# One load instead of two for the first heads' keys and for w_o's first rows, in a decode step on one core

## The chip, the core and the metric

The kernel runs on one core of a Trainium2 chip. A core has a matrix engine (TensorE, in the profile PE, with its weight loads as PEld), a vector engine (VectorE, DVE), a scalar engine (ScalarE, ACT), GpSimd (POOL) and SyncE (SP), which here only waits for semaphores and issues loads. Sixteen DMA engines move the data. The metric is the time of one execution on the device in microseconds (us): the median of several runs.

## What is computed

One token (a row x of 576) goes through two branches, whose results are added to x. Cut to what matters:

```python
xn = layernorm(x)
# A: attention over the last W = 4096 positions of a cache, 32 query heads, 16 key/value heads of 128
q = xn @ wq                                  # wq: 576 x 4096
p = softmax(q . k[last 4096] * 128**-0.5)    # each key head serves two query heads
A = (p . v[last 4096]) @ wo                  # wo: 4096 x 576
# B: gated MLP
z = gelu(xn @ w_in)                          # w_in: 576 x 4608, halves z1 and z2
B = (z1 * (layernorm(z2) * w_sp + b_sp)) @ w_out   # w_out: 2304 x 576
out = x + A + B
```

There is one token, so every weight is used once and every cached key and value by two query heads: 51 MB are read for some 40 million multiplications.

## The kernel before

**Tiles and stages.** The 16 key heads are worked in four stages b = 0 to 3 of four heads each (`NB = 4`, `HB = 4`). The keys of a stage are one tile k0, k1, k2 or k3 of 128 partitions x 32 KB (4096 KB), the values likewise v0 to v3. Of each partition's 128 positions, line 214 (`turn`) transposes 16 at a time, so a stage's keys take eight transposes on VectorE. `scores(b)` multiplies them with the queries on TensorE (line 259), takes the maximum on VectorE (line 262 to 275), the exponential on ScalarE (line 279), and turns the result with a ninth transpose (line 281). `values(b)` multiplies with the values (line 293) and normalizes (line 304). `z_all` and `gate` are the MLP's first half; at the end stand the output rows: o_p (line 375) holds the attention's result, and lines 391 and 399 multiply it with w_o's 32 rows per partition and the gate's hv with w_out's 18.

**Order.** The schedule is written by hand: every engine runs its instructions in program order. The order of the stages is turn 0, scores 0, turn 1, scores 1, values 0, turn 2, scores 2, values 1, turn 3, scores 3, gate, values 2, values 3, then the output rows. VectorE and TensorE alternate inside a stage.

**Loads.** SyncE issues all large loads in the order in which lines 106 to 124 list them: w_q in three pieces, k0 in two halves (line 107), k1, v0, k2, v1, k3, w_in in two, v2, v3, w_o's rows 0 to 13 and 14 to 27 (line 120), its last four rows (wo28), and w_out in five pieces. ScalarE issues three tiny ones (x and two scalars). Large tiles share two buffers, small ones (k0 to k3, v2 and w_o's first 28 rows are of this width) share two more. So a load can have to wait until an earlier tile's readers are done: k2 takes the buffer of k0 and waits for k0's last transpose, k3 that of k1, v1 that of w_q, w_in that of v0, v2 that of k2, v3 that of v1, w_o's first 28 rows that of k3, w_out that of w_in. While SyncE waits for one, all loads behind it wait too.

**Semaphores.** Each load and the store of the result adds to one of eight semaphores on completion; the DMAs take these eight in turn, in the order of the program. A DMA whose turn comes on a semaphore waits until the DMA eight places before it has landed. A reader waits until its load's semaphore has its full count, which is after the whole of that one load. In the profile's records the eight have the numbers 100, 102, 103, 104, 106, 107, 109 and 110. Before, there are 26 DMAs, and the store is the last of them and sits on 102. At the end SyncE waits for all semaphores, two in each instruction, before the closing barrier of the engines.

The names: `load` and `load_kv` cut a tile's columns at `cuts` and issue one DMA for each piece; NU = 128 positions a partition, WR = 32 rows of w_o a partition, D = 576.

Of the kernel before, what the change touches and what calls it, by code (L numbers as in the profile page):

```python
# [15 lines left out]
D = 576  # L16
# [9 lines left out]
NU = W // NJ  # L26
# [11 lines left out]
SMALL = NU * DH  # L38
# [6 lines left out]
def kernel(  # L45
# [38 lines left out]
    def unit(name, width):  # L84
        pool = small if width == SMALL else large
        return pool.tile([P, width], BF16, name=name, tag="u")
# [4 lines left out]
    def load(t, view, width, cuts):  # L91
        for a, e in zip(cuts, cuts[1:]):
            nc.sync.dma_start(t[:, (a - cuts[0]) * width:(e - cuts[0]) * width], view[:, a * width:e * width])  # L93

    def load_kv(cache, name, b, width, cuts=(0, NU)):
        t = unit(f"{name}{b}", width)
        src = cache[0, HB * b:HB * (b + 1), SK - W:SK, :].rearrange("s (j u) d -> j s (u d)", u=NU)
        for a, e in zip(cuts, cuts[1:]):
            nc.sync.dma_start(t[:, a * DH:e * DH], src[:, :, a * DH:e * DH])  # L99
        return t  # L100

    kn, vn = {}, {}
    wq_v, win_v = halves(A_wq), halves(B_w_in)
    wo_v = A_wo.rearrange("(p r) n -> p (r n)", r=WR)
    wq_t = unit("wq", LARGE)
    load(wq_t, wq_v, 2048, (0, 2, 4, NR))
    kn[0] = load_kv(A_k_cache, "k", 0, SMALL, (0, NU // 2, NU))
    kn[1] = load_kv(A_k_cache, "k", 1, SMALL)
    vn[0] = load_kv(A_v_cache, "v", 0, LARGE)
    kn[2] = load_kv(A_k_cache, "k", 2, SMALL)  # L110
# [6 lines left out]
    vn[2] = load_kv(A_v_cache, "v", 2, SMALL)  # L117
    vn[3] = load_kv(A_v_cache, "v", 3, LARGE)
    wo_t = unit("wo", SMALL)
    load(wo_t, wo_v, D, (0, 14, 28))  # L120
    wo28 = one.tile([P, FH], BF16, name="wo28", tag="side")
    load(wo28, wo_v, D, (28, WR))
    wout_t = unit("wout", LARGE)
# [285 lines left out]
    nc.sync.dma_start(out.flatten_outer_dims().rearrange("o (g c) -> (o g) c", g=4), res[0:97:32, :])  # L409


# [1 line left out]
_INS = ['A_x', 'A_k_cache', 'A_v_cache', 'A_wq', 'A_wo', 'B_x', 'B_w_in', 'B_w_sp', 'B_b_sp', 'B_w_out']  # L413
_OUTS = [((1, 1, 576), 'bfloat16')]
# [25 lines left out]
```

## Time and profile before

| | us |
|---|---|
| median of 3 runs (lowest, highest) | 128.26 (128.17, 128.54) |
| the profiled execution's own time | 128.43 |
| its span, first to last instruction | 126.6 |
| busy: TensorE matmul, VectorE, ScalarE | 76.3, 65.6, 10.2 |
| share of 16 DMA engines' span, SyncE's queue | 94.8% |
| SyncE issues k0's halves | 2.09 and 2.87 |
| first transpose of k0, last one's end | 19.12, 28.65 |
| SyncE issues k2 | 28.67 |
| SyncE issues w_o's first piece | 83.19 |
| last load landed | 123.25 |
| SyncE issues the store | 123.97 |

A time in the profile counts from the span's first instruction. The page gives busy time by engine, the busy share of engines and DMA in 40 slices, the DMA queues, and the chain of work that ended last: from the last instruction back, at each step, to what released it. A transfer in this chain counts from its issue to its landing, so that a transfer that waits in the queue behind others is long there. The timeline lists instructions in order, with the idle time of the engine before each and what ended it. SyncE's waits are events of its own sequencer, and their times are in the semaphore records.

### The profile page before, as it was taken

Reading aid. Unit: us, or ns where it says so; the run is one execution under the profiler, and the core shown is the slowest. Engines: PE = TensorE matmul, PEld = TensorE weight load, DVE = VectorE, ACT = ScalarE, POOL = GpSimd, SP = SyncE. Lnnn points to the kernel's source line nnn. Section 1 sums busy time; section 2 is a strip of 40 time slices with the busy share of each in tenths; the row PEclk is TensorE's granted clock in tenths of the full one; section 3 lists DMA queues with packets and bytes.
Section 4 is the critical chain, followed back from the end, with each engine's and each line's share of the span. In section 5 each row is a group of like instructions: output and inputs, shape, how many; then the busy total and the mean of one; then the engine's idle time right before and its main releaser. Section 6 shows DMA issues by size and latency. Waiting matters only on the chain.

```text
span 126.6 us, 1380 instructions
## 1 busy us (share of the span) xinstructions
PE 76.3 (60%) x562; PEld 35.0 (28%) x562; DVE 65.6 (52%) x133; ACT 10.2 (8%) x19; POOL 3.9 (3%) x10
## 2 busy tenths in 40 slices
PE   3241435995179946339963729991960865757470
PEld 3120211331023413313422403330730432423240
DVE  6660069996599844079953169944438400040010
ACT  4010000000300003100003100003000110100010
POOL 8400000000000000000000000000000000000000
PEclk9999999999756999955999975698555595865555
DMA  4999999998998999989999899898999989999930
GB/s 101 427 445 440 430 424 450 430 497 383 448 471 352 476 404 435 476 362 476 404 435 476 382 459 454 384 454 387 487 393 440 455 366 418 433 405 423 400 138 0
DMA packets 3187, 51.03 MB, mean 403 GB/s; under 512 B 365, under 2 KB 622, under 8 KB 1134
## 3 DMA queue, kind: packets, MB, share of 16 engines
q1 hardware_dynamic: 3176, 50.96, 94.8%
q8 instruction: 4, 0.07, 0.2%
q14 instruction: 1, 0.01, 0.0%
q10 hardware_dynamic: 6, 0.00, 0.0%
HBM read 50.96 MB, written 0.00 MB: 402 GB/s over the span
## 4 chain that ended last, share of the span: by engine, by line
DMA 78%; PE 10%; DVE 6%; SPq 2%; ACT 1%; issue 1%; ACTq 0%
DMA k<-in_A_k_cache_dram 37%; DMA v<-in_A_v_cache_dram 27%; DMA wout<-in_B_w_out_dram 14%; PE s L259 8%; DVE kt L214 5%; PE pv L293 1%; ACT p L279 1%; SPq L93 1%; SPq L99 1%; DVE sm L262 1%; PE tr L270 0%; PE su L283 0%; PE fin L399 0%; DVE res L408 0%; DVE m L272 0%
## 5 line engine op out<-in xcount | busy, mean ns | idle before, releaser
L259 PE MATMUL s<-kt,zq 128*128 128x512 bf16 x128 | 38.4, 465 | 10.3 <-DVE kt L214 10.1
L214 DVE STREAM_TRANSPOSE kt<-k 128x1024 f32<-128x1024 f32 x32 | 36.6, 1208 | 3.1 <-DMA k<-in_A_k_cache_dram 3.1
L259 PEld LDWEIGHTS <-zq 128*128 128x128 bf16 x128 | 14.6, 114 | 32.9 <-issue 23.0
L293 PE MATMUL pv<-v,pt 128*32 128x512 bf16 x128 | 10.2, 477 | 1.9 <-DMA v<-in_A_v_cache_dram 1.9
L279 ACT ACTIVATE p<-sm,nm 128x1024 bf16<-128x1024 f32 x4 | 4.6, 1147 | 71.1 <-DVE nm L275 71.1
L304 DVE TENSOR_TENSOR o_t<-op,rm 128x8 bf16<-128x8 f32 x4 | 0.7, 166 | 15.0 <-PE op L301 15.0
L223 PE MATMUL q_ps<-wq,xw 128*32 128x512 bf16 x36 | 4.2, 627 | 6.6 <-DMA wq<-in_A_wq_dram 4.3
L262 DVE CUSTOM_DVE_ANT_1 sm<-s,cm 128x512 f32<-128x512 f32 x8 | 5.4, 672 | 4.7 <-PE s L259 4.7
L281 DVE STREAM_TRANSPOSE pt<-p 128x1024 bf16<-128x1024 bf16 x4 | 5.0, 1245 | 5.4 <-ACT p L279 5.4
L283 PE MATMUL su<-sel,l 128*128 128x8 f32 x8 | 1.8, 293 | 7.6 <-ACT p L279 7.6
L301 PE MATMUL op<-selu,pvs 128*128 128x8 f32 x32 | 4.2, 259 | 2.8 <-ACT pvs L298 2.8
L293 PEld LDWEIGHTS <-pt 128*32 128x32 bf16 x128 | 3.7, 118 | 6.6 <-issue 3.2
L301 PEld LDWEIGHTS op<-selu,pvs 128*128 128x128 f32 x32 | 3.9, 191 | 4.8 <-ACT pvs L298 4.8
L391 PE MATMUL acc<-wo,o_p 128*1 128x288 bf16 x64 | 4.4, 439 | 0.8 <-DMA wo<-in_A_wo_dram 0.8
L395 DVE COPY acc_sb<-acc 128x288 f32<-128x288 f32 x1 | 0.5, 459 | 8.4 <-PE acc L391 8.4
L227 DVE CAST q_sb<-q_ps 128x512 bf16<-128x512 f32 x1 | 0.7, 692 | 7.5 <-PE q_ps L223 7.5
L317 PE MATMUL z<-win,xw 128*32 128x288 bf16 x72 | 4.5, 446 | 0.0
L270 PE MATMUL tr<-ident_f,m 128*128 128x128 f32 x8 | 1.9, 326 | 3.9 <-DVE m L268 3.9
L223 PEld LDWEIGHTS <-xw 128*32 128x32 bf16 x36 | 1.4, 130 | 8.6 <-issue 8.6
L283 PEld LDWEIGHTS su<-sel,l 128*128 128x128 f32 x8 | 1.4, 218 | 8.4 <-ACT p L279 8.4
L298 ACT COPY pvs<-pv 128x512 f32<-128x512 f32 x4 | 2.3, 586 | 13.0 <-PE pv L293 13.0
L346 PE MATMUL sz_ps<-sz,ones_f 128*128 128x2 f32 x2 | 0.6, 362 | 4.6 <-DVE sz L343 4.6
(95 smaller groups left out, 45.1 us busy)
## 6 DMA issues: line engine op xcount, KB each, us to landing
v<-in_A_v_cache_dram SPq DMA_DIRECT2D x4, 4096.0 KB, 32.3
k<-in_A_k_cache_dram SPq DMA_DIRECT2D x3, 4096.0 KB, 30.6
win<-in_B_w_in_dram SPq DMA_DIRECT2D x1, 4608.0 KB, 34.2
k<-in_A_k_cache_dram SPq DMA_DIRECT2D x2, 2048.0 KB, 19.1
wo<-in_A_wo_dram SPq DMA_DIRECT2D x2, 2016.0 KB
wq<-in_A_wq_dram SPq DMA_DIRECT2D x1, 2560.0 KB, 12.6
wq<-in_A_wq_dram SPq DMA_DIRECT2D x2, 1024.0 KB, 6.9
wout<-in_B_w_out_dram SPq DMA_DIRECT2D x1, 1152.0 KB, 25.3
```

The source lines that it names most:

```text
L214: nc.vector.transpose(t[:].rearrange("p c n e -> p (c n e)").bitcast(FP32), kn[b][:, UK * DH * k:UK * DH * (k + 1)].bitcast(FP32).rearrang ...
L223: nc.tensor.matmul(q_ps[32 * g:32 * g + 32, :], lhsT=xw[:, r, :], rhs=wq_t[:, 2048 * r + 512 * g:2048 * r + 512 * (g + 1)], start=r == 0, ...
L259: nc.tensor.matmul(s_ps[:], lhsT=zq[:, b, ce, ZPAD - 8 * k4:ZPAD - 8 * k4 + P], rhs=kt[b, 4 * kk + k4][:, c, :, e], start=k4 == 0 and ce = ...
L262: nc.vector.tensor_tensor_reduce(out=sm[:, kk, :].rearrange("p (n s) -> p n s", s=HB), in0=s_ps[:].rearrange("p (n s) -> p n s", s=HB), in ...
L279: nc.scalar.activation(p[:], sm[:].rearrange("p k n -> p (k n)"), ACT.Exp, bias=nm[:], accum_out=l[:])
L281: nc.vector.transpose(p_t[b][:].rearrange("p k u m -> p (k u m)"), p[:])
L283: nc.tensor.matmul(su[:], lhsT=l[:].to_broadcast([P, P]), rhs=sel8[:], start=True, stop=True)
L293: nc.tensor.matmul(pv[32 * g:32 * g + 32, :].rearrange("p (n d) -> p n d", n=4), lhsT=p_t[b][:, kk, u, :], rhs=v4[:, kk, u, :, :], start=k ...
L298: nc.scalar.copy(pvs[:], pv[:])
L301: nc.tensor.matmul(op[:], lhsT=pvs[:, DH * u:DH * (u + 1)], rhs=selu[:, 8 * u:8 * u + 8], start=u == 0, stop=u == 3)
L317: nc.tensor.matmul(zp[i][32 * g:32 * g + 32, :], lhsT=xw[:, r, :], rhs=rhs, start=r == 0, stop=r == NR - 1, tile_position=(0, 32 * g))
L391: nc.tensor.matmul(acc[i][32 * g:32 * g + 1, :], lhsT=col, rhs=w[:, HW * i:HW * (i + 1)], start=n == 0 and g > 0, stop=n + 4 >= len(rows), ...
```

## The change

Two loads that were issued in two pieces are issued in one. The halves of k0 become one load of 4096 KB, so that its readers wait for one semaphore and for the whole tile. The two 14-row pieces of w_o become one load of 28 rows, 4032 KB. The bytes, the tiles, the buffers and all compute instructions stay. There are 24 DMAs instead of 26; all DMAs behind the first cut move up by one place in the turn of semaphores, those behind the second by two, and the store comes to 110, the last of the eight.

```diff
-    kn[0] = load_kv(A_k_cache, "k", 0, SMALL, (0, NU // 2, NU))
+    kn[0] = load_kv(A_k_cache, "k", 0, SMALL)
...
-    load(wo_t, wo_v, D, (0, 14, 28))
+    load(wo_t, wo_v, D, (0, 28))
```

## The prediction

> **What bounds the kernel now.** I read the page first, then the chain of waits in order of time, then the timeline, then SyncE's closing instructions. The page:
>
> ```profile
> DMA  4999999998998999989999899898999989999930
> q1 hardware_dynamic: 3176, 50.96, 94.8%
> DMA 78%; PE 10%; DVE 6%; SPq 2%; ACT 1%; issue 1%; ACTq 0%
> ```
>
> The second line is the queue of all SyncE's loads: 50.96 MB, and its packets fill 94.8% of the 16 DMA engines' span. The chain names DMA for 78%, and the rest of it is mostly work by which a buffer came free for a load that then waited in a full queue. The chain's DMA pieces and its end:
>
> ```profile
> 2.87 21.13 DMA k<-in_A_k_cache_dram
> 24.02 4.63 DVE kt L214 x4
> 28.67 25.92 DMA k<-in_A_k_cache_dram
> ...
> 71.19 34.61 DMA v<-in_A_v_cache_dram
> 105.80 0.02 issue
> 105.82 17.43 DMA wout<-in_B_w_out_dram
> 123.25 0.04 issue
> 123.29 0.32 PE fin L399 x4
> ```
>
> A load of 4096 KB is issued 26 to 35 us before it lands. Alone it takes 9.71 us: by the semaphore records the loads of k0 (second half), k1, v0, k2, v1 and k3 land at 23.99, 33.70, 44.87, 54.58, 64.30 and 74.01, one behind the other (v0's 11.17 us hold a 1.1 us instruction fetch at 36.8 on one DMA engine, which keeps that engine behind from then on). So the bound is one unbroken stream of loads to 123.25, then a tail of 3.4 us to the span's end at 126.6. The profiled execution took 128.43 us, 1.8 around its span; the median of the runs is 128.26. I take the sum as a difference and subtract it from 128.26.
>
> The places where compute waits for the stream are the slack that the change can use:
>
> ```profile
> 24.02 4.62 DVE L214 STREAM_TRANSPOSE kt<-k 128x1024 f32<-128x1024 f32 x4 [0.27 <-DMA k<-in_A_k_cache_dram]
> 54.61 9.13 DVE L214 STREAM_TRANSPOSE kt<-k 128x1024 f32<-128x1024 f32 x8 [1.91 <-DMA k<-in_A_k_cache_dram]
> 74.03 9.13 DVE L214 STREAM_TRANSPOSE kt<-k 128x1024 f32<-128x1024 f32 x8 [0.94 <-DMA k<-in_A_k_cache_dram]
> 105.85 3.18 PE L293 MATMUL pv<-v,pt 128*32 128x512 bf16 x32 [1.92 <-DMA v<-in_A_v_cache_dram]
> 112.88 1.84 PE L391 MATMUL acc<-wo,o_p 128*1 128x288 bf16 x26
> 115.48 2.56 PE L391 MATMUL acc<-wo,o_p 128*1 128x288 bf16 x38 [0.76 <-DMA wo<-in_A_wo_dram]
> 119.70 1.13 PE L391 MATMUL acc<-wout,hv 128*1 128x288 bf16 x16 [1.65 <-DMA wout<-in_B_w_out_dram]
> 121.48 0.77 PE L399 MATMUL fin<-wout,hv 128*1 128x144 bf16 x20 [0.65 <-DMA wout<-in_B_w_out_dram]
> ```
>
> The bracket is the engine's idle time before the row and what ended it.
>
> **Part 1, two transfers fewer in the stream: -0.15 us.** The halves of k0 land at 19.10 and 23.99, after wq's last piece at 14.21: 4.89 and 4.90 us, together 9.79. The undivided 4096 KB of k1, k2, v1 take 9.71 to 9.72. One cut costs 0.075 us. The packet records say why: a 16384 B packet takes 611 ns, a 32768 B one 1214 to 1219, so two cost 3 to 8 ns more than one, 8 times per DMA engine, and a 4-byte packet of 9 ns ends each transfer. wo's halves take 4.82 each (v3 lands at 105.80, they at 110.62 and 115.44), 9.64; a line through 4096 KB in 9.71 and 576 KB (wo28) in 1.43 gives 9.56 for 4032 KB, again 0.077 less. From below it could be 2 x 0.04 (8 packets x 4 ns + 9), from above 2 x 0.09; I take 0.15. It reaches the end undiminished as long as the queue never runs dry. SyncE's two issues (728 and 333 ns) lie beside the stream.
>
> The Trainium skill (DMA: Bandwidth & Descriptors, Anatomy of one DMA) gives each DMA on the gpsimd queue a fixed part of about 2.0 us besides its bytes; by that as an estimate two fewer would save 4 us. The rows of this stream differ: 0.075 us each.
>
> **Part 2, the store on the last semaphore: -0.19 us.** SyncE's closing waits (L435) are event instructions that each wait for two semaphores, in a fixed order; the eight of the DMAs are 100, 102, 103, 104, 106, 107, 109, 110.
>
> ```profile
> L435 SPq EVENT_SEMAPHORE  x7: 17/28/898, 124.7 to 126.6; - x7
> SPq L435 <- DMA out_dram<-res: 0.9, 1, 0.9
> ```
>
> The semaphore records place them: (104, 103) at 124.68, (106, 102) from 124.75 to 125.64, which is the store's landing (the 898 ns), then (107, 100) at 125.68, (109, 101) at 125.74, (110, 108) at 125.80, the drain at 125.87, and the barrier. The store is the 26th DMA and sits on 102, in the second pair; three pairs pass only after it has landed, 64 ns apart. As the 24th it is on 110, in the last pair: the other four pairs take 4 x 64 = 0.26 us while the store is in flight (0.9), and the drain follows at once. Saved: 3 x 0.064 = 0.19. From below 0 (if the order of pairs changes with the counts), from above 0.26; I take 0.19 because the pairs run 3-2, 4-1, 5-0 and then 6 and 7 with engines' semaphores, an order that depends on the semaphores and not on the loads.
>
> **Part 3, k0 in one piece: VectorE starts 4.9 us later, at no cost.** Line 214's first transposes run from 19.12 on the first half. Now all eight wait for the whole, which lands at 23.92. Eight take 9.1 us (34.33 to 43.40 in k1's turn), so k0's turn ends at 33.1 instead of 28.65. What is late next: k2's load, queued behind that wait on SP with v1 behind it, is issued at 33.1 instead of 28.67; by then k1 is just landing and v0 (until 44.8) still lies ahead, so the queue stays full with 11 us to spare. scores(0)'s rest behind the transposes costs 6.3 (43.33 to 49.67 in stage 1), so k1's turn starts at 39.4 instead of 34.33, ends at 48.5, releases k3's load at 48.5 instead of 43.43 (v1 is ahead of it until 64.2), and values(0) ends 9.2 behind that: 57.7. There 1.91 us of waiting are eaten: k2's turn starts at 57.7 instead of 54.61, 3.1 late; k3's at 76.25 instead of 74.03, 2.2 late (0.94 eaten). The loads these release (win 56.0, v2 66.9, v3 74.4, wo 85.4, wo28 and wout 96.2 to 98.5) each find at least 7 us of stream ahead of them. The gate and values(2) are 2.2 late; values(3), which waited 1.92 for v3, starts at 106.2 instead of 105.85, so o_p is ready at 112.0 instead of 111.7. wo's second half landed at 115.44: 3.3 us of slack are left. The cover is the stream; without it the price would be the 4.9 itself.
>
> The loads' own waits get easier: a DMA waits until the one eight places before it has landed. v0 waited 1.5 us for wq's first piece (issued at 5.68) and now waits for x_row; wout's last piece waited for v3 (105.80) and now for v2. All lie behind a full queue: nothing.
>
> **Part 4, wo's 28 rows in one piece: 26 matmuls move behind 115.3, at no cost.** The first rows ran 112.88 to 114.72 on the first half. Now all 64 start when the whole lands at 115.3: 1.84 + 2.56 = 4.4 us at the granted clock of 0.50 that holds from 111.9 to the end, so they cannot run at a lower one that the trace has shown. They end at 119.7 against wout's first piece at 119.66 - 0.15 = 119.5: 0.2 late. PE then waits 0.65 before 121.48, and acc_sb, copied by 121.34, is first read at 122.04. Both covers hold it. From above, at the 71 ns apiece of the 26 (1.84 us) and of wout's 16 (1.13 us), 64 take 4.5 us and end 0.3 late, still under the 0.65.
>
> **The sum.** 0.15 + 0.19 = 0.34 us: the last wout lands at 123.10, the span ends at 126.28, and the time is 128.26 - 0.34 = **127.92 us**, 0.27% less.
>
> **Rivals.**
> - Only one half of the gain. The store's wait isn't the last (stream alone: 128.26 - 0.15 = 128.11), or the stream's gain is lost in the trailing DMA engine (tail alone: 128.07). For it: the pairing order is inferred from one kernel. Against: the 64 ns steps. This is also the case that the change doesn't do what it says. Chance 0.12.
> - Slower: k0's late start reaches the output matmuls. Its place is o_p (line 375) against wo's landing; it decides from 3.3 us more delay than I count. If the 4.9 us came through whole, o_p is ready at 116.6, the 64 matmuls end at about 121.9, wout's 16 at 123.0, the copies at 123.5, and 0.7 + 1.0 of line 399 follow: 125.2 instead of 123.6, so 1.6 - 0.34 = +1.3, 129.5 us. For it: DVE and PE alternate in a fixed order, and PE's granted clock falls to 0.5 in stretches of 6.8 us that may now fall on other stages. Against: 1.91, 0.94 and 1.92 us of waits in the rows. The Trainium skill (Trainium Kernel Development and Optimization, Best Practices) asks for loads that overlap compute, and this change takes such an overlap away. Chance 0.06.
> - Slower by a fetch: PE's last instruction fetch (16384 B at 119.0, 1.0 us) moves later with line 391 and meets the DMA engine that is last at 123.25: +1.0 - 0.34, 128.9 us. In the last wout load eleven engines have landed by 121.78 and five trail at 122.41, 122.92, 123.04, 123.17 and 123.25: as many as there were fetches in the span (one of 8192 B, four of 16384 B), so they hit five different engines. Chance 0.04.
> - A larger gain: an exposed start of a DMA. wq's first piece, with nothing ahead of it, needed 4.93 us from issue to landing where the next 1024 KB took 2.43; two such starts fewer would give 5.0, 123.3 us. A full queue speaks against it; 0.01. A smaller one is that the last fetch now misses the stream: down to 127.6; 0.05.
>
> **Chances.** Forecast 0.72. About 0.3% (0.38 us, under 127.88) is what a measurement of this kernel can tell from no change; the forecast lies 0.04 short of it, so I put 0.38 of its chance below and 0.34 inside. Faster: 0.38 + 0.06 = 0.44. Same: 0.34 + 0.12 + 0.02 of the slower cases where they stop early = 0.48. Slower: 0.08. The range 127.6 to 128.3 takes in the bounds of parts 1 and 2 (0.08 to 0.44 saved) and the half gain, and leaves out some 2 in 10.
>
> **What would show it.** The first transposes start at 23.9 to 24.0 and run eight in a row; k2's load is issued near 33.1. Waits of DVE for k2 and k3 vanish. DMA share stays at 9 in every slice. PE's wait for wo ends near 115.3 and takes all 64 rows. The last wout lands near 123.1. The 898 ns wait is the fifth of SyncE's closing pairs, and the drain follows within 0.05 us of it. I am wrong if a load lands later than before, if PE idles less than 0.2 us before line 399, or if pairs still follow the store's landing.

## The result, and the profile after

| | before | after |
|---|---|---|
| median, us (lowest to highest, 10 runs each) | 128.42 (128.17 to 128.54) | 127.87 (127.80 to 128.11) |
| ratio, 95% interval | | 0.9965 (0.9957 to 0.9973) |
| profiled execution: span, us | 126.6 | 126.1 |
| w_q's last piece landed, us | 14.21 | 14.11 |
| last load landed, us | 123.25 | 122.94 |
| store landed, us | 125.62 | 125.25 |

The kernel is 0.35% faster, 0.45 us by the ratio (0.34 to 0.55; the medians lie 0.55 apart); 0.34 us (0.27%) were forecast, at the edge of that interval. Ratios, here and below, leave out executions over 1.5% above their kernel's fastest, which only e7_late_4 has, six of its twelve. First the page of the changed kernel: DMA's busy share by slice, SyncE's queue, and the chain that ended last.

```profile
DMA  4999999898998989999899999899999899999940
q1 hardware_dynamic: 2888, 50.96, 94.8%
PE 42%; DMA 36%; DVE 10%; ACT 5%; SPq 3%; issue 1%; ACTq 0%
```

The stream is as full as before (94.8%), with 288 packets fewer. The chain now names TensorE for 42% where it named DMA for 78%. That isn't a new bound. The chain in order of time, near its end:

```profile
92.48 3.67 PE z L317 x72
...
96.16 0.33 SPq L93
...
98.68 0.43 SPq L93
99.11 0.04 issue
99.16 23.78 DMA wout<-in_B_w_out_dram
122.94 0.04 issue
122.98 0.26 PE fin L399 x4
```

The last load's issue came at 99.16, behind line 317, whose matmuls free w_in's buffer, and then it lay 23.78 us in a full queue. The chain follows who released the issue, and so walks through compute that had 20 us to spare. The queue's share and the full slices say what bounds.

VectorE's turns and TensorE's last part, from the timeline:

```profile
23.85 9.13 DVE L214 STREAM_TRANSPOSE kt<-k 128x1024 f32<-128x1024 f32 x8 [4.75 <-DMA k<-in_A_k_cache_dram]
38.67 9.07 DVE L214 STREAM_TRANSPOSE kt<-k 128x1024 f32<-128x1024 f32 x8
60.15 9.12 DVE L214 STREAM_TRANSPOSE kt<-k 128x1024 f32<-128x1024 f32 x8
78.46 9.12 DVE L214 STREAM_TRANSPOSE kt<-k 128x1024 f32<-128x1024 f32 x8
107.26 3.44 PE L293 MATMUL pv<-v,pt 128*32 128x512 bf16 x32
115.23 4.01 PE L391 MATMUL acc<-wo,o_p 128*1 128x288 bf16 x64 [0.61 <-DMA wo<-in_A_wo_dram]
119.44 1.13 PE L391 MATMUL acc<-wout,hv 128*1 128x288 bf16 x16 [0.20 <-DMA wout<-in_B_w_out_dram]
121.21 0.48 PE L399 MATMUL fin<-wout,hv 128*1 128x144 bf16 x20 [0.64 <-DMA wout<-in_B_w_out_dram]
```

After 23.85 no turn waits for keys any more: k1's, k2's and k3's turns carry no bracket. The waits of 1.91 and 0.94 us are eaten, as is that before line 293. TensorE still waits for w_o, 0.61 us, so the delay ends there. SyncE's closing instructions and its wait for the store:

```profile
L436 SPq EVENT_SEMAPHORE  x7: 17/28/28, 124.3 to 126.0; - x7
SPq L436 <- DMA out_dram<-res: 0.7, 1, 0.7
```

Minimum, median and maximum were 17, 28 and 898 ns and are now 17, 28 and 28. The wait for the store isn't gone. Before, the store's 102 was the second semaphore of its pair, and the wait lay inside that instruction (898 ns). Now 110 is the first of its pair, and the wait lies ahead of the instruction, from 124.53 to 125.27. The semaphore records place the pairs:

| | pairs before the store's | store landed | pairs behind it | drain | from landing to drain |
|---|---|---|---|---|---|
| before | (104, 103) | 125.62 | (107, 100), (109, 101), (110, 108) | 125.87 | 0.25 |
| after | (104, 103) to (109, 101) | 125.25 | none | 125.33 | 0.08 |

So the span's 0.53 us are: 0.09 at the start (w_q's last piece landed sooner), 0.22 in the stream from there to the last load (109.04 us before, 108.82 after), 0.06 from the last load to the store's issue (0.72, now 0.66), and 0.17 behind the store's landing.

### The profile page after: what moved, and what is told of

The parts are those of the page before. It is cut to its first block, busy times and chain, and to the rows that moved or that the text cites. A ratio compares the mean times of both kernels' runs of the same rounds, so it can differ in the third digit from the quotient of the medians.

```text
span 126.1 us, 1377 instructions
## 1 busy us (share of the span) xinstructions
PE 77.6 (62%) x562; PEld 36.3 (29%) x562; DVE 65.3 (52%) x133; ACT 10.2 (8%) x19; POOL 3.9 (3%) x10
## 3 DMA queue, kind: packets, MB, share of 16 engines
q1 hardware_dynamic: 2888, 50.96, 94.8%
## 4 chain that ended last, share of the span: by engine, by line
PE 42%; DMA 36%; DVE 10%; ACT 5%; SPq 3%; issue 1%; ACTq 0%
PE s L259 30%; DMA wout<-in_B_w_out_dram 19%; DMA k<-in_A_k_cache_dram 17%; PE pv L293 4%; ACT p L279 4%; DVE kt L214 4%; SPq L93 3%; PE z L317 3%; PE op L301 2%; DVE sm L262 2%; PE tr L270 2%; PE su L283 1%; DVE pt L281 1%; DVE m L272 1%; ACT pvs L298 1%
## 5 line engine op out<-in xcount | busy, mean ns | idle before, releaser
L259 PE MATMUL s<-kt,zq 128*128 128x512 bf16 x128 | 37.4, 460 | 11.9 <-DVE kt L214 11.9
L293 PE MATMUL pv<-v,pt 128*32 128x512 bf16 x128 | 12.6, 563 | 0.0
L301 PE MATMUL op<-selu,pvs 128*128 128x8 f32 x32 | 5.9, 311 | 2.8 <-ACT pvs L298 2.8
L301 PEld LDWEIGHTS op<-selu,pvs 128*128 128x128 f32 x32 | 5.5, 259 | 5.8 <-ACT pvs L298 5.8
L317 PE MATMUL z<-win,xw 128*32 128x288 bf16 x72 | 3.7, 382 | 0.0
```

Of the source, the lines that this page charges most:

```text
L259: nc.tensor.matmul(s_ps[:], lhsT=zq[:, b, ce, ZPAD - 8 * k4:ZPAD - 8 * k4 + P], rhs=kt[b, 4 * kk + k4][:, c, :, e], start=k4 == 0 and ce = ...
L293: nc.tensor.matmul(pv[32 * g:32 * g + 32, :].rearrange("p (n d) -> p n d", n=4), lhsT=p_t[b][:, kk, u, :], rhs=v4[:, kk, u, :, :], start=k ...
L301: nc.tensor.matmul(op[:], lhsT=pvs[:, DH * u:DH * (u + 1)], rhs=selu[:, 8 * u:8 * u + 8], start=u == 0, stop=u == 3)
L317: nc.tensor.matmul(zp[i][32 * g:32 * g + 32, :], lhsT=xw[:, r, :], rhs=rhs, start=r == 0, stop=r == NR - 1, tile_position=(0, 32 * g))
```

## The experiments

The landing times below are from the semaphore records. "Stream" is the time from the landing of w_q's last piece to that of the last load, "tail" from the store's landing to the drain. A load is spread over the 16 DMA engines, and it has landed when the last of them is done; "mean" is the stream taken from the mean of the 16 engines' landings to the same mean of the last load, so that it doesn't hang on one engine. Theory T is the forecast's: 0.077 us for each cut, about 0.06 for each pair that passes behind the store's landing, and everything else covered. Rival S puts the gain into the semaphore's place alone, rival C into k0's late start.

| kernel | ratio (95%) | median, us | w_q landed | stream | mean | tail |
|---|---|---|---|---|---|---|
| before (first profile) | | 128.42 | 14.21 | 109.04 | 108.02 | 0.25 |
| after (first profile) | 0.9965 (0.9957 to 0.9973) | 127.87 | 14.11 | 108.82 | 107.86 | 0.08 |
| e1_k0_only | 0.9990 (0.9981 to 0.9999) | 128.22 | 14.05 | 108.92 | 107.94 | 0.19 |
| e2_wo_only | 0.9984 (0.9976 to 0.9993) | 128.11 | 14.00 | 109.06 | 107.95 | 0.19 |
| e3_store_only | 0.9989 (0.9980 to 0.9997) | 128.13 | 14.21 | 109.10 | 108.02 | 0.08 |
| e4_stream_only | 0.9976 (0.9967 to 0.9985) | 127.98 | 14.14 | 108.79 | 107.68 | 0.25 |
| e5_cuts_32 | 1.0021 (1.0011 to 1.0030) | 128.67 | 14.29 | 109.55 | 108.49 | 0.08 |
| e6_late_1 | 0.9971 (0.9961 to 0.9982) | 128.11 | 14.19 | 108.94 | 107.87 | 0.08 |
| e7_late_4 | 1.0008 (0.9982 to 1.0035) | 130.18 | 14.17 | 108.85 | 107.87 | 0.08 |
| e8_wq_one | 0.9969 (0.9958 to 0.9981) | 128.01 | 14.13 | 108.78 | 107.67 | 0.08 |
| e9_k0_late | 0.9984 (0.9976 to 0.9993) | 128.14 | 14.13 | 108.87 | 107.82 | 0.25 |
| e10_wo_late | 0.9995 (0.9986 to 1.0004) | 128.29 | 14.01 | 109.13 | 108.01 | 0.25 |
| e11_after_again | 0.9963 (0.9950 to 0.9976) | 127.85 | 14.05 | 108.81 | 107.86 | 0.08 |
| e12_before_again | 1.0002 (0.9993 to 1.0011) | 128.35 | 14.07 | 109.05 | 108.02 | 0.25 |

The mean follows T's 0.077 a cut: two cuts fewer give 0.15 or 0.16 us (after, e6, e7, e11), one fewer 0.08 (e1) and 0.07 (e2), six more 0.47 (e5), and none 0.00 or 0.01 (e3, e10, e12). Three kernels lie some 0.2 us lower than T has them, e4, e8 and e9; see at k0 only late.

**One cut alone, k0's.** The diff is the change's first line only.

```diff
-    kn[0] = load_kv(A_k_cache, "k", 0, SMALL, (0, NU // 2, NU))
+    kn[0] = load_kv(A_k_cache, "k", 0, SMALL)
```

> Only k0 comes in one load; w_o's first 28 rows stay in two. 25 DMAs, the store on semaphore 100, in the third of the five closing pairs. Theory T (a cut costs the stream 0.077 us, and each closing pair that passes after the store's landing costs 0.06): k0 lands 0.08 earlier than before relative to w_q's last piece, the stream stays 0.08 ahead to its end, two pairs follow the store's landing instead of three, 0.14 us less than before in all (ratio 0.9989). Rival S (all of the gain comes from the semaphore's place, cuts cost nothing): 0.06 less (0.9995). Rival C (the late start of k0's turn, by what it moves on TensorE and in the instruction fetches, makes the gain): most of the 0.45, 0.3 to 0.45 less (0.9965 to 0.9977).

0.13 us less (0.01 to 0.24): T's number. C's 0.3 lies outside the interval, S's 0.06 doesn't. k0 lands 9.72 us after w_q, where the halves needed 9.79. Two pairs follow the store's landing, and the tail is 0.19.

**The other cut alone, w_o's.**

```diff
-    load(wo_t, wo_v, D, (0, 14, 28))
+    load(wo_t, wo_v, D, (0, 28))
```

> Only w_o's first 28 rows come in one load; k0 stays in halves, so its first transposes start near 19.1 us again. 25 DMAs, the store on semaphore 100. Theory T: w_o's 28 rows land 0.08 sooner after v3 than before, the end of the stream 0.08 sooner, two pairs behind the store's landing, 0.14 us less than before (ratio 0.9989). Rival S: 0.06 less (0.9995). Rival C: the same 0.06 or less, since nothing is late; the line-391 matmuls still start on the whole load near 115.3.

0.20 us less (0.09 to 0.31), 0.14 expected. The last landing came no sooner in this profile (a stream of 109.06), where T had 0.08; the mean of the 16 did, by 0.07. Another 0.06 lie between the last load and the store's issue (0.66 us instead of 0.72), which T didn't have. w_o's 28 rows land 9.59 us after v3, where the halves needed 9.64, and the tail is 0.19. Both rivals' 0.06 lies outside the interval of 0.09 to 0.31, as S and C gave it here.

**The store's place alone.** Two tiny loads leave, so the count comes to 24 with all cuts in place. A constant 1 stands for both scalars, w_sp and b_sp: the kernel leaves that part of the computation out.

```diff
-    nc.scalar.dma_start(ws2[:, 0:1], B_w_sp.flatten_outer_dims()[0:1, 0:1])
-    nc.scalar.dma_start(ws2[:, 1:2], B_b_sp.flatten_outer_dims()[0:1, 0:1])
...
+    nc.gpsimd.memset(ws2[:], 1.0)
```

> All cuts as before; the two 2-byte loads of w_sp and b_sp are left out and a constant 1 is used for both (that part of the computation is left out), so the program has 24 DMAs and the store is on 110. Theory T: the stream ends as before (last load 123.1 to 123.3), no pair follows the store's landing, 0.17 to 0.19 us less than before (ratio 0.9986). Rival S: the whole 0.45 less (0.9965). If the pairs' order had nothing to do with it: no change.

0.14 us less and a tail of 0.08, with the stream as before (109.10). The closing instructions of this kernel, same columns as above, against those of the next one:

```profile
L434 SPq EVENT_SEMAPHORE  x7: 17/28/28, 124.7 to 126.5; - x7
SPq L434 <- DMA out_dram<-res: 0.7, 1, 0.7
```

S falls: the place alone makes a third of the gain, and v0's issue at 4.16 us instead of 5.68 brings the stream nothing.

**The cuts gone, the store's place as before.** Two tiny loads more, into a tile that nobody reads.

```diff
+    ws3 = const.tile([1, 2], BF16, name="ws3")
+    nc.scalar.dma_start(ws3[:, 0:1], B_w_sp.flatten_outer_dims()[0:1, 0:1])
+    nc.scalar.dma_start(ws3[:, 1:2], B_b_sp.flatten_outer_dims()[0:1, 0:1])
```

> Both loads whole as in the changed kernel, and two more 2-byte loads on ScalarE's queue into a tile that nobody reads, so that there are 26 DMAs and the store is back on 102, in the second pair. Theory T: the stream ends 0.15 us sooner than before, three pairs follow the store's landing again, 0.15 us less than before (ratio 0.9988). Rival S: no change (1.0000). Rival C: what k0's late start makes is all here, 0.27 less or more (0.9979).

```profile
L439 SPq EVENT_SEMAPHORE  x7: 17/28/904, 124.3 to 126.2; - x7
SPq L439 <- DMA out_dram<-res: 0.9, 1, 0.9
```

The long wait (904 ns) stands among the seven again, three pairs follow it, and the tail is back at 0.25. But the gain is 0.31 us (0.19 to 0.42) where T had 0.15. That is more than T allows, and what C foresaw; see below at k0 only late.

**Six cuts more than before, the store on 110.** The diff cuts k0 at each quarter, w_o at 7, 14 and 21, and k1 and v0 in the middle.

> The kernel before with six cuts more: k0 and w_o's 28 rows in four pieces each, k1 and v0 in two. 32 DMAs, so the store is on 110 as in the changed kernel, with eight cuts more than there. Theory T (0.077 us a cut): the stream ends 0.5 us later than before (6 x 0.077), the tail saves 0.17, in sum 0.3 us more than before (ratio 1.0023) and 0.6 more than the changed kernel. Rival S (cuts cost nothing): 0.17 to 0.45 less than before (0.9965 to 0.9987).

0.27 us more than before, 0.30 expected, and S falls a second time. In the stream k0's quarters take 2.48, 2.48, 2.49 and 2.49 us, together 9.94 against 9.71 whole: 0.077 for each of three cuts. w_o's take 9.82 against 9.58 to 9.60: 0.07 to 0.08 each. The whole stream is 0.51 longer for six cuts. This is the cleanest measurement of the term.

**How much delay the cover holds.** k0's last transpose is done n + 1 times, for n = 1 and n = 4.

```diff
-            nc.vector.transpose(
...
+            for _ in range(2 if b == 0 and k == 7 else 1):
+                nc.vector.transpose(
```

> The changed kernel with k0's last transpose done twice, which makes VectorE 1.1 us later from k0's turn on; nothing else changes. If the cover before the output rows is what the changed kernel's trace shows (TensorE waits 0.6 us for w_o, 0.2 for w_out's first piece and 0.64 before line 399), 1.1 us are hidden: the changed kernel's time (ratio 0.9965 to before), with TensorE's wait for w_o gone. If the cover was the 3.3 us of the prediction: the same time, and TensorE still waits for w_o.

> The changed kernel with k0's last transpose done five times, 4.6 us later. With a cover of 1.5 to 2 us the rest comes through: 2.5 to 3.1 us more than the changed kernel (ratio 1.016 to 1.021 to before). With the 3.3 us of the prediction: 1.3 more (1.007). If the stream alone set the time: no change.

TensorE's last part with one transpose more:

```profile
114.97 0.70 PE L384 MATMUL acc<-x_row,one_bf 1*1 1x288 bf16 x2 [0.80 <-DVE acc L382]
115.60 4.01 PE L392 MATMUL acc<-wo,o_p 128*1 128x288 bf16 x64
119.65 1.13 PE L392 MATMUL acc<-wout,hv 128*1 128x288 bf16 x16
```

The wait for w_o is gone, the 64 matmuls start at 115.60 instead of 115.23, and the time is the changed kernel's within the interval. With four more the time depends on the execution: 127.95 to 131.72 us in twelve runs, where no other kernel here scatters by more than 0.5. The ratio of 1.0008, from the six fastest, misses the 1.016 to 1.021 expected; the median of all twelve, 130.18, lies 2.3 us above the changed kernel's. The profiled one, the fastest, still hides the 4.6 us:

```profile
112.90 1.06 PE L302 MATMUL op<-selu,pvs 128*128 128x8 f32 x8 [0.69 <-ACT pvs L299]
...
116.06 4.01 PE L392 MATMUL acc<-wo,o_p 128*1 128x288 bf16 x64
119.86 1.18 PE L392 MATMUL acc<-wout,hv 128*1 128x288 bf16 x16
```

Its mean granted clock was 0.82. The spans go with that clock: 126.2 to 126.8 us in the five runs at 0.82 to 0.85, 127.9 to 129.1 in the five at 0.813 to 0.815, 129.2 and 129.9 in the two at 0.79. That suggests that the cover isn't one number but what the granted clock leaves of it, and that 4.6 us are too much for most executions. It isn't shown: there is no profile of a longer run to say where its time went.

**w_q in one load as well.** It would beat both kernels if T held at the start of the stream too.

```diff
-    load(wq_t, wq_v, 2048, (0, 2, 4, NR))
+    load(wq_t, wq_v, 2048, (0, NR))
```

> The changed kernel with w_q in one load instead of three, and two more 2-byte loads into a tile that nobody reads, so that there are 24 DMAs and the store stays on 110. The query matmuls start only at 14 us, two us later than they end now, before k0 lands at 23.7, where VectorE waits 4.75 us. Theory T: the stream ends 0.15 us sooner than in the changed kernel, 0.15 less than it (ratio 0.9953 to before). Rival S: the changed kernel's time (0.9965).

A miss: the changed kernel's time, not 0.15 less, although this kernel's large tiles were moved as well (see the next experiment). w_q whole lands at 14.13, in the middle of the 14.00 to 14.29 that the three pieces need in the other profiles. The cuts that come first save nothing measurable. In the other profiles the first packets that the engines take are drawn out (8192 B in up to 1.3 us, 309 ns later on), so a saving there would be lost in the start's scatter. Behind w_q the mean of the 16 falls to 107.67, as in e4_stream_only, but the last engine lands hardly sooner than in the changed kernel (108.78 against 108.82).

**k0 only late, w_o only late.** The first adds a copy ahead of k0's turn that reads the second half; the second takes w_o's rows 14 to 27 first.

```diff
+    late_k = const.tile([P, 1], BF16, name="late_k")
+    nc.vector.tensor_copy(late_k[:], kn[0][:, SMALL - 1:SMALL])
     turn(0)
```

> The kernel before, with both cuts and the store on 102, and one small VectorE copy that reads the last column of k0's second half ahead of k0's turn. So VectorE starts k0's turn near 24.0 us, as in the changed kernel, and nothing else of the change is there. Theory T: a covered delay, the time of the kernel before (ratio 1.0000, within 0.0008). Rival C (the late start itself makes the gain that was found over the forecast): 0.1 to 0.16 us less (0.9988 to 0.9992), with the last load landing 0.1 sooner after w_q's last piece than in the kernel before (under 108.95 us, against 109.04).

> The kernel before, with both cuts and the store on 102, but line 391 takes w_o's rows 14 to 27 first and 0 to 13 behind them, so that all 64 matmuls start only when the second piece has landed, as in the changed kernel. Theory T: the time of the kernel before (ratio 1.0000). If running all rows in one go raises the clock that TensorE is granted behind the last load: 0.05 us less (0.9996) and the clock at 1.0 from 120 us on.

```profile
23.95 0.16 DVE L356 COPY late_k<-k 128x1 bf16<-128x1 bf16 x1 [4.84 <-DMA k<-in_A_k_cache_dram]
24.02 9.12 DVE L214 STREAM_TRANSPOSE kt<-k 128x1024 f32<-128x1024 f32 x8
```

VectorE is as late as in the changed kernel, and the kernel is 0.20 us faster (0.09 to 0.31) with a stream of 108.87: what C foresaw and T did not. But this kernel differs in one more thing. The new tile takes 32 bytes a partition and moves all large tiles behind it: w_in's ninth piece and wo28 from byte 45536, which is 32 above a multiple of 64, to 45568, which is one. The same holds for e4_stream_only and e8_wq_one, and for no other kernel here. In the packet records, median ns of a packet and time of wo28's load behind the one before it (mean landing of the first eight DMA engines):

```
kernel             4608 B   9216 B   3456 B   wo28's load
before                181      352      136   1.42 us
after                 181      352      136   1.42 us
e1_k0_only            181      352      136   1.43 us
e9_k0_late            178      347      135   1.37 us
e4_stream_only        178      347      135   1.36 us
```

w_in's ninth piece likewise takes 1.36 instead of 1.42 us, and w_out's third 1.05 instead of 1.09. The three together are 0.15 us. That is about what these two kernels gained over T (0.16 in e4_stream_only, 0.20 in e9_k0_late). The times alone don't tell, since the changed kernel, not moved, also gained 0.28 apart from its tail. The mean of the 16 landings separates the two. Four kernels are late and not moved (after, e1_k0_only, e6_late_1, e7_late_4), and their means are T's within 0.01 us, however late VectorE is. The three that were moved lie 0.19 to 0.20 us below T's. So the late start brings the stream nothing, C falls, and the extra goes with the move. That the address alone makes it would take a kernel with the tile and nothing else, which was not run.

w_o only late changes nothing that can be measured (0.9995, interval over 1), and the clock behind the last load is 0.5, not 1.0, so the finer reason for that run isn't borne out either.

**Both kernels again.**

> The changed kernel unchanged, for a second profile and more timed rounds on the same chip as the two before it. Theory T as forecast: 0.34 less than before (ratio 0.9973), of it 0.17 behind the store's landing. If the first measurement stands: 0.9965. Time from w_q's last piece to the last load: 108.82 in the first profile; T says 108.89 (109.04 less 0.15).

> The kernel before unchanged, for a second profile: it says how far the same program's landing times scatter. Ratio 1.0000. If the start of the stream scatters by itself, w_q's last piece lands 0.05 to 0.2 us away from 14.21 us, and the time from there to the last load lies within 0.1 of 109.04.

The stream is 109.05 us before and 108.81 after, within 0.01 of the first profiles, and w_q lands at 14.07 and 14.05: the 0.09 at the start is scatter, since the kernel before has 14.07 in one profile and 14.21 in the other. The ratio of 0.9963 confirms the first. TensorE's last part in the second profile of the changed kernel:

```profile
112.37 0.58 PE L383 MATMUL acc<-x_row,one_bf 1*1 1x288 bf16 x2 [0.80 <-DVE acc L381]
115.12 4.01 PE L391 MATMUL acc<-wo,o_p 128*1 128x288 bf16 x64 [2.17 <-DMA wo<-in_A_wo_dram]
```

Here the wait for w_o is 2.17 us, where the first had 0.61: the same program, another course of the clock.

## Why the prediction was right, and where its sizes were off

**What bounds** held: the stream ends the kernel, and compute keeps off the path, with a chain that looked otherwise.

**Part 1, the stream** held in mechanism and sign. A cut costs 0.077 us, measured on k0's and w_o's quarters, and the 0.075 of the forecast came from the right rows. As a term of the sum it was mis-sized: 0.15 were forecast, and the stream became 0.22 shorter, then 0.24 (109.05 to 108.81). 0.07 to 0.09 are left over. They sit in the DMA engine that lands last: the mean of all 16 gains 0.16 in both pairs of profiles, which is the two cuts, and the last engine trails the mean of the first eight by 1.80 and 1.85 us before, 1.70 and 1.66 after. In e1_k0_only, also late and not moved in address, it trails by 1.71, in e6_late_1 by 1.83. Why instruction fetches hold that engine up less in the changed kernel isn't shown; over all kernels the trail scatters from 1.66 to 1.92, so the 0.07 to 0.09 may be luck. The Trainium skill (DMA: Bandwidth & Descriptors, Anatomy of one DMA) has about 2.0 us of fixed cost for one DMA on the gpsimd queue. The quarters on SyncE's full queue show 0.08.

**Part 2, the tail** held: 0.19 forecast, 0.17 measured in both profiles, and in order with the pairs behind the landing: 0.25 with three, 0.19 with two, 0.08 with none. The 64 ns a pair were a little much: 0.17 / 3 is 56 ns.

**Part 3, k0's late start** was covered as said. The turns started at 38.7, 60.2 and 78.5, where 39.4, 57.7 and 76.25 were forecast. The step that failed is the size of the cover, 3.3 us left at o_p. It left out VectorE's clearing of fin and acc and TensorE's first two matmuls (113.4 to 114.6), which lie between o_p and w_o, and took before's durations for values(0) and values(2). At a granted clock of 0.5 line 301 took 1.87 us in both instead of 1.06, and line 293 3.60 in values(0) instead of 1.91. Measured are 0.61 and 2.17 us of waiting. In the second profile, where values(0) ran at the full clock (1.91 and 1.06 us), the turns start at 38.6, 57.1 and 76.3, near the forecast: there the clearing and the two matmuls alone make the difference from 3.3 to 2.17. The rival of the late start reaching the output may have been nearer than its 0.06 said, if the longer runs with four transposes more are that rival, which no profile shows.

**Part 4, the 64 matmuls** held: 4.01 us instead of 4.4, and a wait of 0.20 us ahead of w_out's first piece where 0.2 late was forecast.

**What was not in the sum:** 0.06 us between the last load and the store's issue. Both profiles of the changed kernel have a granted clock of 1.0 there, both of the kernel before 0.5; line 399's last four matmuls take 0.26 us instead of 0.32. Among the others, e2, e4, e7 and e8 have 0.66 and e1, e3, e5, e6, e9 and e10 have 0.72. So six of the seven profiles with w_o's 28 rows whole have 0.66, and none of the seven with them in pieces; it isn't the 64 matmuls in one go, which e10 has too. The cause stays open. With these 0.06, 0.16 + 0.17 + 0.06 = 0.39 us are accounted for, inside the measured 0.34 to 0.55.

The rival of the fetch that meets the last engine didn't occur: five fetches, five trailing engines again. The rival of half the gain falls with e3 and e5: the store's place alone gains 0.14 us, and six cuts more lengthen the stream by 0.5.

## What to carry to other kernels

Where one queue is full from start to end, cost a cut in a load by the stream, packet by packet (here 0.08 us for each), and ask what the cut buys: a head start that the next full wait swallows buys nothing. Look behind the last transfer too: in which place the closing waits take its semaphore was worth 0.17 us and no work at all. How far the last DMA engine trails the others scatters by 0.26 us over these profiles; the mean of all 16 shows a term of 0.08. When an experiment adds so much as a small tile, compare the addresses and packet times of everything behind it before the result is put down to what was meant.

## What the runs showed of the hardware that was not expected

- A shift of all large tiles by 32 bytes, to multiples of 64, goes with packets that are 1 to 2% shorter: 181 to 178 ns for 4608 B, 352 to 347 for 9216 B. The mean of the 16 landings is 0.19 to 0.20 us lower in the three kernels that have the shift. Packets of 32768 B (1213 to 1218 ns) and 5760 B (220) hardly change with it. The Trainium skill (DMA: Bandwidth & Descriptors, How a descriptor splits into AXI transactions) says that a descriptor that doesn't start on a 256-byte boundary costs extra beats. It says so of reads, and here the place that is written moved. The 4608 B rows (byte 224 of 256 before, 0 after) agree in direction, but w_out's 9216 B rows start at byte 96 and then 128 of 256 and got shorter too.
- Instruction fetches of 16384 B, four in a span, hold up one DMA engine each by some 1.2 to 1.6 us, and the last to land sets the end. They go with TensorE's progress: before the fetches at 36.8, 73.2, 96.4 and 119.0 us it had begun 187, 483, 698 and 997 matmuls and weight loads, and in e7_late_4, where they come at 47.5, 82.7, 102.2 and 120.1, 186, 480, 694 and 1004. The Trainium skill (Runtime: NRT & Kernel Launch, Instruction fetch mechanics) has blocks of 16 KiB or 256 instructions, fetched ahead, and the cost as mostly hidden. The blocks' size agrees; here their time on the DMA engine is not hidden, since loads fill it.
- The granted clock of TensorE followed a different course in two executions of the same program (0.60 and 0.86 on the mean from 50 to 62 us for the changed kernel), and with it the slack of compute: 0.61 and 2.17 us.
